# The second FFN layer of four pairs of token tiles as 2x2 block products with seven products instead of eight

## The chip, the cores and the metric

One core of a Trainium2 chip runs the program. It has five engines with queues of their own: PE (matmuls; PEld is its weight load), DVE (vector), ACT (activations), POOL (a second vector engine that reads and writes SBUF but not PSUM) and SP, which here only starts DMAs. The metric is the device time of one execution in microseconds (us); a difference of 0.3% (0.7 us) is about what a measurement can tell from no change.

## The reference

```
P = sort_net; five rounds of softmax over rows, then division by the column sums
k_sorted = einsum('bhij,bhjcd->bhicd', P, k_b)          # the same for v
attn = softmax(q_b @ k_sorted^T / 8);  x = attn @ v_sorted   # 32 groups of 96 tokens, 8 heads
h = x @ w_in                                            # 3072 x 512 by 512 x 2048
g = max(h, 0) + alpha * min(h, 0)
out = g @ w_out                                         # 3072 x 2048 by 2048 x 512, float32
```

## The kernel before

Tokens come in four batches of 768, each batch in eight groups of 96. For each group g attention is computed over all eight heads (`attention(g)`), for the next batch keys and values are mixed in between (`conv_k`, `prep_k`, `conv_v`, `prep_v`; the `conv` steps are copies into zero-padded tiles KSz and VDz, from the second batch on by POOL). Four groups make a chunk of 384 tokens. For each chunk `ffn1` computes 16 blocks of the hidden layer, one for each 128 of the 2048 columns: four matmuls of 384 columns into one of two PSUM banks (psH), an ACT instruction into a tile t1 (`t<-psH`), and a DVE instruction (SCALAR_TENSOR_TENSOR, STT below) that writes the block as bf16 into hT. hT is laid out [128 columns of the hidden layer, 16 blocks, ring of 768 tokens], so two chunks stand in it.

`ffn2` is the second layer. It works on tiles of 128 tokens, 24 in all. One tile is 16 matmuls that add up in one PSUM bank: the stationary operand is a 128x128 piece of hT, the moving one is a block row of w_out, 128 x 512. The bank is then copied to one of four tiles outstg by ACT or DVE, and SP stores it (256 KB). The banks are the two halves of psYP (keys psY and PSP), and the two of psS from tile 21 on. The last tile, 23, is made as two halves of 256 columns, in psS and psO, so that its last copy and store are short.

The order of work is not left to chance: every step is recorded in a graph (`_Graph.add`, with what it reads and writes), and the table `SEQ` holds one list of step numbers, with a letter where a step that several engines could do is given to one of them (p, a, d). `arrange` hands each engine its steps in that order; `emit` adds the semaphore waits. So each engine runs a fixed list, and an instruction that waits holds up everything behind it on its engine. The steps of the second layer come from `ffn_plan`, in the main part of the function.

Of the kernel before, what the change touches and what calls it, by code (L numbers as in the profile page):

```python
# [61 lines left out]
830 838 797 814 798 846 815d 818 799 839 844 800 831 845 804 819 821 820 864 822 771 848 865 772 832 874 849d  # L62
847 824 823 875 833 825 710 850 826 827 834d 851 872 648 828 805 852 873 829 883 853 675 866 854 876 855 877d
701 858 806 807d 856 878 867 884 859 879 860 885 773 857 840 898 841 880 835 899 861 774 881 944 882 862 900
863 892 842d 889 868 893 886 890 808 894 945 869 891 870 887d 756 924 895 925 901 912 896 926 897 888 913 871
906 843 909 950 910 902 951 739 907 946 903 914 908 952 927 911 918 904d 921 794 919 915 953 922 920 923 970
809 932 971 935 933 916d 947 936 934 972 937 981 938 928 973 939 941 940 996 942 982 905 943 958 997 961 959
929 948d 983 962 960 998 963 984 930d 964 985 967 999 1022 968 954 1023 965 1042 955 1010 969 1024 956d 1043
966 957 974 987 975 976d 931 978 988 1011 989 979 986 980 1048 949 993 1049 977 990 994 1012 995 991 917 992
1025 1007 1004 1008 1044 1009 1005 1050 1006 1019 1016 1000 1020 1013 1051 1001 1017 1021 1068 1018 1045 1002d  # L70
1033 1014d 1046 1003 1030 1069 1034 1026 1031 1079 1027 1035 1070 1032 1080 1028d 1039 1071 1036 1040 1081
1041 1037 1029 1038 1052 1059 1053 1054d 1082 1060 1055 1061 1056 1083d 1100 1057 1084 1058 1065 1047 1062
1066 1124 1067 1063 1064 1085 1072 1086 1076 1087 1125 1077 1073 1074 1078 1091 1088 1101 1092 1075 1089 1093
1126 1090 1015 1097 1094 1098 1102 1099 1095 1096 1109 1106 1110 1127 1111 1107 1108 1115 1112 1116 1103 1117
1113 1114 1121 1104d 1118 1122 1166 1119 1120 1172 1123 1130 1133 1131 1145 1134 1135 1146 1132 1139 1136 1140
1184 1141 1137 1167 1138 1151 1142 1152 1147 1153 1143 1144 1173 1128d 1157 1129 1154 1105 1158 1148 1159 1155
1156 1163 1149 1168 1150 1164 1165 1160 1185 1161 1174 1162 1186 1169 1187 1170 1175 1188 1189 1178 1171 1176
1179 1177 1180 1181 1182 1183
# [231 lines left out]
def bass_sinkhorn_attn__then__act_prelu_kernel(  # L310
# [48 lines left out]
    omaT = sb("omaT", [128, 16], F32)  # L359
# [111 lines left out]
    def consts():  # L471
# [6 lines left out]
        G.add(DVE, lambda e: e.memset(sel0[:, :, :], 0.0), 420, w=["sel0"], prio=-87)  # L478
# [24 lines left out]
        for n in range(NE):  # L503
# [19 lines left out]
        G.add(ACT, lambda e: copy(e, AP(selk, 0, [[512, 32], [16, 32], [1, 16]]),  # L523
                                  AP(identf, 0, [[128, 32], [1, 32], [0, 16]])), 600,
              r=["identf"], w=["selk"], prio=-66)
        G.add(ACT, lambda e: copy(e, AP(sel0, 0, [[1024, 32], [16, 8], [130, 8], [1, 2]]),
                                  AP(identf, 0, [[128, 32], [1, 8], [0, 8], [0, 2]])), 300,
              r=["identf"], w=["sel0"], prio=-66.5)
        return ib.idx
# [35 lines left out]
    def spread0(prio):  # L565
        def f(e):
            inst = None
            for j in range(8):
                inst = e.matmul(psYP[:, 1, 0:8], AP(sel0, j * 128, [[1024, 32], [1, 128]]),
                                AP(Pb, j, [[64, 32], [8, 8]]), start=(j == 0), stop=(j == 7))  # L570
            return inst
        G.add(PE, f, 300, r=["Pb", "sel0"], w=PSP, prio=prio)
        G.add(DVE, lambda e: e.tensor_tensor(
            out=AP(BDK, 0, [[512, 128], [16, 8], [2, 8], [1, 2]]),
            in0=AP(mkh, 0, [[16, 128], [2, 8], [0, 8], [1, 2]]),
            in1=AP(psYP, 512, [[1024, 128], [0, 8], [1, 8], [0, 2]]), op=AluOpType.mult), 330,
            r=PSP + ["mkh"], w=[("BDK", 0)], prio=prio)

    def spread(bs, prio):
        n = len(bs)  # L580
        late = bs[0] > 0
        rows = n * (1 + late)

        def f(e):
            inst = None
            for x in range(n):
                inst = e.matmul(psYP[:, 1, x * 64:x * 64 + 64], AP(selk, bs[x] * 128, [[512, 32], [1, 128]]), Pb[:, :])
            for x in range(n * late):
                for hf in range(2):
                    inst = e.matmul(AP(psYP, hf * 64 * 1024 + 512 + (n + x) * 64, [[1024, 64], [1, 64]]),  # L590
                                    AP(selk, bs[x] * 128, [[512, 32], [2, 64]]), Pb[:, :])
# [12 lines left out]
        for x, b in enumerate(bs):  # L604
            G.add(SMALL, lambda e, x=x, b=b: e.tensor_tensor(
                out=AP(BDM, b * 64, [[256, 128], [16, 4], [2, 8], [1, 2]]),
                in0=AP(mkhM, 0, [[8, 128], [2, 4], [0, 8], [1, 2]]),
                in1=AP(dsel, x * 8, [[48, 128], [0, 4], [1, 8], [0, 2]]), op=AluOpType.mult), {"dve": 220, "pool": 420},
                r=["dsel", "mkhM"], w=[("BDM", b)], prio=prio) if late else G.add(DVE, lambda e, x=x, b=b: e.tensor_tensor(
                out=AP(BDK, b * 128, [[512, 128], [16, 8], [2, 8], [1, 2]]),  # L610
                in0=AP(mkh, 0, [[16, 128], [2, 8], [0, 8], [1, 2]]),
                in1=AP(dsel, x * 8, [[48, 128], [0, 8], [1, 8], [0, 2]]), op=AluOpType.mult), 260,
                r=["dsel", "mkh"], w=[("BDK", b)], prio=prio)
        for x, b in enumerate(bs if late else []):
            G.add(SMALL, lambda e, x=x, b=b: e.tensor_tensor(
                out=AP(BDV, b * 64, [[256, 128], [8, 8], [1, 8]]),
                in0=AP(mkhV, 0, [[8, 128], [1, 8], [0, 8]]),
                in1=AP(dsel, (n + x) * 8, [[48, 128], [0, 8], [1, 8]]), op=AluOpType.mult), {"dve": 220, "pool": 420},
                r=["dsel", "mkhV"], w=[("BDV", b)], prio=prio + 0.5)
# [312 lines left out]
                  dma=(d_o[ob + x], 0))  # L932


    G.add(DVE, lambda e: e.memset(bz[:, :], 0.0), 100, w=["bz"], prio=-120)

    def burst(e):
# [41 lines left out]
    for ga, gb in chunks:  # L979
# [110 lines left out]
```

## Time and profile before

| | |
|---|---|
| runs | 234.4, 235.03, 235.07 us; median 235.03 |
| profiled execution | 232.5 us from its first to its last instruction; no other time of it is given |
| PE | busy 221.9 us (95%), 2516 matmuls recorded |
| weight loads | 139.3 us (60%) |
| DVE, ACT | 166.5 us (72%), 157.6 us (68%) |
| POOL | 102.7 us (44%), all of it before 141.4 us |
| granted TensorE clock | 1.000 |

A row of a group of instructions reads: line of the program, engine, operation, what it writes <- what it reads, sizes, count | busy us, mean ns of one | idle time of the engine before them and what ended it. The mean time of a matmul is its latency; matmuls overlap, so what one takes of PE is read from the distance of their starts.

### The profile page before, as it was taken

To read this page: it belongs to the slowest core of one execution; us is meant where nothing else is said; L and a number is where in the kernel's file an instruction comes from. 1 tells how busy PE (TensorE), PEld (TensorE's weight loads), DVE (VectorE), ACT (ScalarE), POOL (GpSimd) and SP (SyncE) were. 2 spreads that over 40 slices of the span, in tenths; PEclk is the share of its full clock that TensorE was granted. 3 is DMA by queue.
4 is the path that set the end of the run, shared out by engine and by line. 5 is a ranking of instruction groups with operands and counts; after the bars stand their busy time and mean duration, and the time that the engine had idled before them with its cause. 6 is when DMAs were issued, how large, how long until landed. Compare 5 with 4: busy or idle time off the path is not lost.

```text
span 232.5 us, 6278 instructions
## 1 busy us (share of the span) xinstructions
PE 221.9 (95%) x2516; PEld 139.3 (60%) x2543; DVE 166.5 (72%) x342; ACT 157.6 (68%) x435; POOL 102.7 (44%) x149
## 2 busy tenths in 40 slices
PE   3998999999999999999999999999999999999995
PEld 3456588685666656665665666555555555555553
DVE  5659599896898978696688677758677675463540
ACT  4369667889989596757888587686684764642332
POOL 7999239859076995863999932000000000000000
PEclk9999999999999999999999999999999999999999
DMA  5999999996996699999749998678515533200033
GB/s 70 218 209 197 215 205 186 184 192 116 192 183 124 64 123 170 172 193 206 155 104 137 107 110 181 131 178 171 97 34 143 116 57 121 63 0 0 10 128 135
DMA packets 73389, 31.36 MB, mean 135 GB/s; under 512 B 64512, under 2 KB 68368, under 8 KB 73360
## 3 DMA queue, kind: packets, MB, share of 16 engines
q0 software_dynamic: 24816, 13.63, 43.3%
q1 hardware_dynamic: 48544, 17.33, 37.1%
q8 instruction: 20, 0.33, 0.6%
q14 instruction: 9, 0.07, 0.1%
HBM read 27.28 MB, written 6.29 MB: 144 GB/s over the span
## 4 chain that ended last, share of the span: by engine, by line
PE 76%; POOL 11%; DMA 9%; issue 2%; ACT 0%; POOLq 0%
PE psH L875 32%; PE psYP L915 29%; DMA KS<-in_k_dram 9%; PE psS L915 4%; PE psS L756 3%; POOL KSz L655 3%; PE psO L813 3%; PE psYP L709 2%; PE psYP L668 2%; POOL VDz L401 1%; POOL QN L491 1%; POOL w_in_bf L960 1%; PE psO L915 1%; POOL QN L431 1%; PE psO L848 1%
## 5 line engine op out<-in xcount | busy, mean ns | idle before, releaser
L889 DVE SCALAR_TENSOR_TENSOR hT<-t,omaT,psH 128x384 bf16<-128x384 f32 (+1 forms) x140 | 76.7, 565 | 30.2 <-ACT t L885 29.4
L875 PE MATMUL psH<-xT,w_in_bf 128*128 128x384 bf16 (+1 forms) x560 | 96.9, 310 | 0.3 <-DVE hT L889 0.3
L885 ACT ACTIVATE t<-psH 128x384 f32<-128x384 f32 x126 | 60.6, 494 | 42.9 <-PE psH L875 42.3
L915 PE MATMUL psYP<-w_out_bf,hT 128*128 128x512 bf16 x309 | 78.4, 379 | 1.4
L875 PEld LDWEIGHTS psH<-xT,w_in_bf 128*128 128x128 bf16 x560 | 50.1, 98 | 29.2 <-DVE hT L889 2.7
L793 ACT ACTIVATE Esb<-psS,nf 96x96 bf16<-96x96 f32 x192 | 46.2, 344 | 2.1 <-DVE nf L765 2.0
L915 PEld LDWEIGHTS psYP<-w_out_bf,hT 128*128 128x128 bf16 x336 | 30.5, 98 | 28.1
L401 POOL COPY VDz<-VST 64x384 bf16<-64x384 bf16 x40 | 33.9, 848 | 16.4 <-PE psH L875 6.5
L655 POOL COPY KSz<-KS 64x512 bf16<-64x512 bf16 x36 | 22.1, 613 | 16.5 <-DMA KS<-in_k_dram 8.0
L765 DVE TENSOR_REDUCE nf<-psS 96x8 f32<-96x768 f32 x24 | 22.8, 950 | 8.9 <-PE psS L756 8.6
L431 POOL DMA_DIRECT2D QN<-in_q_dram x24 | 19.9, 846 | 0.7 <-POOL QN L491 0.6
L826 DVE TENSOR_TENSOR xq<-psO,rec 96x512 bf16<-96x512 f32 x27 | 18.4, 683 | 0.5
L813 PEld LDWEIGHTS psO<-VS,ET 112*128 112x128 bf16 x248 | 11.1, 98 | 3.4 <-ACT xT L401 0.5
L813 PE MATMUL psO<-VS,ET 112*128 112x65 bf16 x248 | 12.7, 194 | 0.0
L756 PEld LDWEIGHTS psS<-KT,QTz 128*128 128x128 bf16 (+1 forms) x192 | 10.7, 101 | 3.3 <-ACT Esb L793 0.2
L756 PE MATMUL psS<-KT,QTz 128*128 128x96 bf16 (+1 forms) x192 | 12.2, 206 | 0.0
L401 DVE CAST VS<-psYP 112x512 bf16<-112x512 f32 x15 | 10.3, 689 | 2.3 <-PE psYP L709 2.3
L821 DVE RECIPROCAL rec<-psO 96x8 f32<-96x8 f32 x31 | 6.2, 200 | 6.1 <-PE psO L813 5.7
L709 PEld LDWEIGHTS psYP<-BDV,VDz 128*128 128x128 bf16 x192 | 8.3, 98 | 3.3 <-POOL VDz L401 0.4
L401 ACT ACTIVATE outstg<-psYP 128x512 f32<-128x512 f32 x11 | 6.6, 603 | 5.0 <-PE psYP L915 4.9
L915 PE MATMUL psS<-w_out_bf,hT 128*128 128x512 bf16 (+1 forms) x48 | 9.8, 344 | 0.0
L709 PE MATMUL psYP<-BDV,VDz 128*128 128x64 bf16 x192 | 9.5, 193 | 0.1
(139 smaller groups left out, 209.6 us busy)
## 6 DMA issues: line engine op xcount, KB each, us to landing
out_dram<-outstg SPq DMA_DIRECT2D x23, 256.0 KB, 2.6
KS<-in_k_dram POOLq DMA_DIRECT2D x3, 768.0 KB, 9.1
QN<-in_q_dram POOLq DMA_DIRECT2D x24, 96.0 KB, 3.8
w_in_bf<-in_moe_w_in_dram POOLq DMA_DIRECT2D x4, 512.0 KB, 16.7
w_out_bf<-in_moe_w_out_dram POOLq DMA_DIRECT2D x2, 1024.0 KB, 18.5
VST<-in_v_dram POOLq DMA_DIRECT2D x4, 384.0 KB, 10.1
hT<-in_q_dram POOLq DMA_DIRECT2D x1, 768.0 KB, 7.3
VST<-in_v_dram POOLq DMA_DIRECT2D x1, 768.0 KB, 13.1
```

The source lines that it names most:

```text
L401: return e.activation(o, i, ACTF.Copy) if e is nc.scalar else e.tensor_copy(o, i)
L431: G.add(POOL, lambda e, h=h: e.dma_start(AP(QN, h * 128 + (h // 4) * 64, [[6144, 128], [1024, 6], [1, 64]]), AP(q.tensor, b * HB + h * S * ...
L655: G.add(POOL, lambda e, hp=hp: e.tensor_copy(AP(KSz, hp * 64 * 3072 + u % 3 * 1024 + hp * 64, [[3072, 64], [128, 8], [1, 64]]), AP(KS[n], ...
L709: inst = e.matmul(AP(t, off + dd * 64, [[row, 128], [1, 64]]), AP(VDz, (u % VSL * 8 + dd) * 128, [[VSL * 1024, 128], [1, 128]]), AP(BDV, b ...
L756: inst = e.matmul(o, AP(QTz[n], hp * 3072 + h4 * 768 + i * 96, [[6144, 128], [1, w]]), AP(KT[n], (h4 * 8 + i) * bk, [[ld, 128], [64, 2], [ ...
L765: G.add(DVE, lambda e: e.tensor_reduce(AP(nx, 0, [[8, 96], [4, 2], [1, 4]]), AP(psX, 0, [[1024, 96], [512, 2], [96, 4], [1, 96]]), AxisLis ...
L793: inst = e.activation(AP(Esb[me], p * 128, [[1024, 96], [64, 2], [1, 48]]), AP(psX, (p // 4) * 512 + (p % 4) * 96, [[1024, 96], [48, 2], [ ...
L813: inst = e.matmul(AP(psZ, hp * 512 + h4 * 68, [[1024, 128], [1, 65]]), AP(ET[me] if far else ET[m], pos(h4, hp) * 96, [[800, nk], [1, 128] ...
L875: inst = e.matmul(AP(pt, poff + x * n, [[1024, 128], [1, n]]), AP(w_in_bf, kt * DFF + (ft + x) * 128, [[KT_TILES * DFF, 128], [1, 128]]), ...
L885: G.add(ACT, lambda e: e.activation(AP(t1[tb], 0, [[384, 128], [1, k * n]]), AP(pt, poff, [[1024, 128], [1, k * n]]), ACTF.Relu, scale=-1. ...
L889: G.add(DVE, lambda e, x=x: e.scalar_tensor_tensor(out=AP(hT, (ft + x) * RING + tok % RING, [[FT_TILES * RING, 128], [1, n]]), in0=AP(t1[t ...
L915: inst = e.matmul(AP(bank[0], bank[1], [[1024, 128], [1, n]]), AP(hT, ft * RING + tok % RING, [[FT_TILES * RING, 128], [1, 128]]), AP(w_ou ...
```

## The change

Tiles 13+14, 16+17, 19+20 and 22+23 are taken as pairs a and b. For a pair the product is a 2x2 block product: the two tiles are the block rows; the even and the odd blocks of the hidden layer are the two halves of the inner dimension; the columns 0-255 and 256-511 of w_out are the block columns. Strassen's scheme (in Winograd's form) needs seven block products in place of eight. Each has eight matmuls of 256 columns, so a pair takes 56 matmuls of 256 columns where two tiles took 32 of 512.

For it there are four sums of blocks of w_out, made once (`w_sums`, eight instructions of 128x1024 bf16 elements, as each is cut in two halves), in SBUF that is free by then: KS[0] and VST[0], which held keys and values of the third batch, and a tile WT3, which takes the place of sel0 and selk and holds these until then. And for each pair there are four sums of blocks of hT (`strassen`, S1 to S4, eight instructions of 128x512 bf16), in QTz[0] or VDz. The seven products add up in psYP; in between its first quarter is copied to SBUF three times (`snap`) and added to other quarters on the way to outstg (`total`, DVE). The numbering of steps is new, and SEQ is new from about its last two fifths on, for all engines.

```diff
-775 783 777 811 784 786 778d 615 836 785 787 791 620 788 779 792 614 780d 837 617 795 793 781 616 796 770 782d
...
+775 783 777 811 784 786 778d 615 836 785 787 791 620 788 779 792 614 780d 837 795 781 804 793 782d 796 797 798
...
-    selk = sb("selk", [32, 4, 128], BF16)
+    WT3 = sb("WT3", [128, 8, 256], BF16)
...
-    sel0 = sb("sel0", [32, 8, 128], BF16)
...
+    PAIRS = [13, 16, 19, 22]
...
+    def wt(n, j):
+        if n == 3:
+            return WT3, 2048, j * 256
+        t, off = (((KS, VST)[n - 1][0], j * 256) if n < 3 else ((KS, VST)[j // 4][0], 2048 + j % 4 * 256))
+        return t, 3072, off
+
+    def w_sums():
...
+                G.add(SMALL, f, {"dve": 800, "pool": 2150},
+                      r=[("w_out", hf)] + [("WT", y, hf)] * isinstance(y, int),
+                      w=[("WT", n, hf)] + (["selk", "sel0"] if n == 3 else old[n - 1] if n < 3 else old[hf]),
+                      prio=-1)
...
+    def strassen(ta, prio):
...
+        for hf in range(2):
+            for n, x, y, op in ((1, (1, 0), (1, 1), AluOpType.add), (2, 1, (0, 0), AluOpType.subtract),
+                                (3, (0, 0), (1, 0), AluOpType.subtract), (4, (0, 1), 2, AluOpType.subtract)):
...
+                    return e.tensor_tensor(out=sv(n, hf), in0=i[0], in1=i[1], op=op)
+                G.add(SMALL, f, {"dve": 520, "pool": 1180}, r=r, w=[("S", m, n, hf)] + first, prio=prio + n / 100)
...
+        def snap(x):
+            G.add(EITHER, lambda e: copy(e, AP(sn, so + x * 256, [[sld, 128], [1, 256]]), AP(psYP, 0, [[1024, 128], [1, 256]])),
...
+        def total(o, n, off, x, keys):
+            G.add(DVE, lambda e: e.tensor_tensor(
+                out=o, in0=AP(psYP, off, [[1024, 128], [256, n], [1, 256]]),
+                in1=AP(sn, so + x * 256, [[sld, 128], [0, n], [1, 256]]), op=AluOpType.add),
...
+        product(0, ["psY"], True, ((0, 0), (0, 0)))
+        product(512, PSP, True, ((0, 1), (1, 0)))
+        snap(0)
+        total(outstg[oa][:, 0:256], 1, 512, 0, [("out", oa)])
+        product(0, ["psY"], False, (2, 2))
+        product(512, PSP, True, ((1, 1), 4))
+        product(768, PSP, False, (1, 1))
+        snap(1)
+        product(0, ["psY"], False, (3, 3))
+        snap(2)
+        total(outstg[ob][:, :], 2, 512, 2, [("out", ob), ("out", ob, 1)])
+        store(tb, ob)
+        product(768, PSP, False, (4, (1, 1)))
+        total(outstg[oa][:, 256:512], 1, 768, 1, [("out", oa, 1)])
+        store(ta, oa)
...
+            if tile_done + x in PAIRS:
+                ffn_plan.append((prios[0], 2, (tile_done + x, prios[0])))
+            if tile_done + x in PAIRS or tile_done + x - 1 in PAIRS:
+                continue
```

The diff's `SMALL` means DVE or POOL. By the new table POOL gets all eight sums of w_out and 25 of the 32 sums of hT, DVE the other seven. Up to the first engine's change the lists are the same: on PE for 231 rows, on DVE 211, on POOL 81.

On POOL, the end of the list before, from the last loads of Q (QN) on: the six copies of keys for the fourth batch.

```order
L655 COPY KSz<-KS1 64x8x64
L401 COPY VDz<-VST1 64x8x48
L655 COPY KSz<-KS1 64x8x64
L431 DMA QN<-in_q_dram 128x6x64 x5
L655 COPY KSz<-KS1 64x8x64 x6
```

The same place now; L957 is `w_sums`, L994 the sums of hT, here for the pair 13+14.

```order
L435 DMA QN<-in_q_dram 128x6x64 x5
L957 TENSOR_TENSOR KS0<-w_out_bf 128x1024
L659 COPY KSz<-KS1 64x8x64
L957 TENSOR_TENSOR KS0<-w_out_bf 128x1024
L659 COPY KSz<-KS1 64x8x64 x5
L994 TENSOR_TENSOR QTz0<-hT 128x512
L957 TENSOR_TENSOR VST0<-w_out_bf,KS0 128x1024
L957 TENSOR_TENSOR KS0<-w_out_bf,VST0 128x1024
L994 TENSOR_TENSOR QTz0<-hT 128x512
L957 TENSOR_TENSOR VST0<-w_out_bf,KS0 128x1024
L994 TENSOR_TENSOR QTz0<-hT,QTz0 128x512
L957 TENSOR_TENSOR VST0<-w_out_bf,VST0 128x1024
```

Two sums of w_out stand ahead of the copies of keys, and where POOL had nothing left it now goes on with sums, to near the end of the program.

On PE, the end of the list before (L875 is `ffn1`, L915 `ffn2`):

```order
L875 MATMUL psH<-xT,w_in_bf 128x384 x4
L915 MATMUL psO<-w_out_bf,hT 128x256 x4
L915 MATMUL psS<-w_out_bf,hT 128x512 x4
L915 MATMUL psO<-w_out_bf,hT 128x256 x4
L915 MATMUL psS<-w_out_bf,hT 128x512 x4
L915 MATMUL psO<-w_out_bf,hT 128x256 x4
L915 MATMUL psS<-w_out_bf,hT 128x512 x4
L915 MATMUL psS<-w_out_bf,hT 128x256 x16
```

The same place now, from the last `ffn1` on (L919 is `ffn2`, for tile 21; L1013 the products of the pair 22+23, whose sums of hT stand in VDz):

```order
L879 MATMUL psH<-xT,w_in_bf 128x384 x8
L1013 MATMUL psYP<-w_out_bf,hT 128x256 x4
L919 MATMUL psS<-w_out_bf,hT 128x512 x4
L1013 MATMUL psYP<-w_out_bf,hT 128x256 x12
L1013 MATMUL psYP<-VST,VDz 128x256 x8
L1013 MATMUL psYP<-KS,hT 128x256 x4
L1013 MATMUL psYP<-VST,hT 128x256 x4
L1013 MATMUL psYP<-WT,VDz 128x256 x8
L1013 MATMUL psYP<-KS,VDz 128x256 x8
L919 MATMUL psS<-w_out_bf,hT 128x512 x8
L1013 MATMUL psYP<-w_out_bf,VDz 128x256 x8
```

Half of tile 21 has moved to just before the last product.

On DVE, the end of the list before:

```order
L401 COPY outstg3<-psYP 128x512
L889 SCALAR_TENSOR_TENSOR hT<-t12,omaT,psH 128x384
L889 SCALAR_TENSOR_TENSOR hT<-t11,omaT,psH 128x384 x2
L889 SCALAR_TENSOR_TENSOR hT<-t10,omaT,psH 128x384
L401 COPY outstg3<-psO 128x256
```

The same place now, from the last two STTs on (COPY to KSz is a `snap`, L1027 a `total`):

```order
L893 SCALAR_TENSOR_TENSOR hT<-t10,omaT,psH 128x384
L893 SCALAR_TENSOR_TENSOR hT<-t11,omaT,psH 128x384
L994 TENSOR_TENSOR VDz<-hT 128x512
L405 COPY KSz<-psYP 128x256
L994 TENSOR_TENSOR VDz<-VDz,hT 128x512
L1027 TENSOR_TENSOR outstg2<-psYP,KSz 128x256
L405 COPY KSz<-psYP 128x256
L1027 TENSOR_TENSOR outstg3<-psYP,KSz 128x512
L994 TENSOR_TENSOR VDz<-hT,VDz 128x512
L405 COPY outstg1<-psS 128x512
L1027 TENSOR_TENSOR outstg2<-psYP,KSz 128x256
```

One short copy behind the last STT has become nine instructions, two of which (the first L994 and the first COPY) stand ahead of the first product of sums on PE. The last store is now a whole tile of 256 KB, where it was half a tile.

More of the change, by code (lines that the diff above doesn't have):

```diff
@@ L65 @@
[L65 to L74, printed above, removed]
@@ L477, in consts @@
                    prio=-84)
-        G.add(DVE, lambda e: e.memset(sel0[:, :, :], 0.0), 420, w=["sel0"], prio=-87)
+        G.add(DVE, lambda e: e.memset(AP(WT3, 512, [[2048, 32], [1, 1024]]), 0.0), 420, w=["sel0"], prio=-87)
         G.add(DVE, lambda e: e.memset(P32[:, 64:72], EPS), 100, w=["eps"], prio=-89)
@@ L522, in consts @@
               220, r=["one0"], w=[("VS1", 0)], prio=-60)
-        G.add(ACT, lambda e: copy(e, AP(selk, 0, [[512, 32], [16, 32], [1, 16]]),
+        G.add(ACT, lambda e: copy(e, AP(WT3, 0, [[2048, 32], [16, 32], [1, 16]]),
                                   AP(identf, 0, [[128, 32], [1, 32], [0, 16]])), 600,
               r=["identf"], w=["selk"], prio=-66)
-        G.add(ACT, lambda e: copy(e, AP(sel0, 0, [[1024, 32], [16, 8], [130, 8], [1, 2]]),
+        G.add(ACT, lambda e: copy(e, AP(WT3, 512, [[2048, 32], [16, 8], [130, 8], [1, 2]]),
                                   AP(identf, 0, [[128, 32], [1, 8], [0, 8], [0, 2]])), 300,
@@ L568, in f @@
             for j in range(8):
-                inst = e.matmul(psYP[:, 1, 0:8], AP(sel0, j * 128, [[1024, 32], [1, 128]]),
+                inst = e.matmul(psYP[:, 1, 0:8], AP(WT3, 512 + j * 128, [[2048, 32], [1, 128]]),
                                 AP(Pb, j, [[64, 32], [8, 8]]), start=(j == 0), stop=(j == 7))
@@ L586, in f @@
             for x in range(n):
-                inst = e.matmul(psYP[:, 1, x * 64:x * 64 + 64], AP(selk, bs[x] * 128, [[512, 32], [1, 128]]), Pb[:, :])
+                inst = e.matmul(psYP[:, 1, x * 64:x * 64 + 64], AP(WT3, bs[x] * 128, [[2048, 32], [1, 128]]), Pb[:, :])
             for x in range(n * late):
@@ L932, in ffn2, with f, at @@
                   dma=(d_o[ob + x], 0))
+    def wt(n, j):
[4 more added lines that the diff above has]
+    def w_sums():
+        w = lambda ft, h: AP(w_out_bf, ft * DM + h * 256, [[FT_TILES * DM, 128], [2 * DM, 4], [1, 256]])
+        old = [("KS", 0)], [("VST", 0)] + [("VST", 0, x) for x in range(4)]
+        for n, x, y, op in ((1, (0, 1), (0, 0), AluOpType.subtract), (3, (1, 1), (0, 1), AluOpType.subtract),
+                            (2, (1, 1), 1, AluOpType.subtract), (4, (1, 0), 2, AluOpType.subtract)):
+            for hf in range(2):
+                def f(e, n=n, x=x, y=y, hf=hf, op=op):
+                    def at(v):
+                        if isinstance(v, tuple):
+                            return w(8 * hf + v[0], v[1])
+                        t, ld, off = wt(v, 4 * hf)
+                        return AP(t, off, [[ld, 128], [256, 4], [1, 256]])
+                    return e.tensor_tensor(out=at(n), in0=at(x), in1=at(y), op=op)
+                G.add(SMALL, f, {"dve": 800, "pool": 2150},
+                      r=[("w_out", hf)] + [("WT", y, hf)] * isinstance(y, int),
+                      w=[("WT", n, hf)] + (["selk", "sel0"] if n == 3 else old[n - 1] if n < 3 else old[hf]),
+                      prio=-1)
@@ L997, in bass_sinkhorn_attn__then__act_prelu_kernel @@
                     ffn1(*a, pr)
+            elif kind == 2:
+                if a[0] == PAIRS[0]:
+                    w_sums()
+                strassen(*a)
             else:
```

81 lines of the change are left out of this document (73 added, 8 removed).

## The prediction

> **What bounds the kernel now.** I read the page first (engines, clock), then the stretch in which the lists differ, cut into stages, then the chain that ended last.
>
> ```profile
> span 232.5 us, 6278 instructions
> PE 221.9 (95%) x2516; PEld 139.3 (60%) x2543; DVE 166.5 (72%) x342; ACT 157.6 (68%) x435; POOL 102.7 (44%) x149
> core 0: us, PE busy (x) PEld busy (x) DVE busy (x) ACT busy (x) POOL busy (x), PEclk, DMA share, GB/s
> 134.00:160.00 26.00, 25.78 (x230) 15.44 (x233) 18.36 (x33) 20.09 (x72) 3.66 (x6) 1.00 0.79 149
> 160.00:180.00 20.00, 19.89 (x151) 11.49 (x152) 15.12 (x26) 12.48 (x39) 0.00 (x0) 1.00 0.47 107
> 180.00:200.00 20.00, 19.84 (x141) 11.22 (x143) 12.93 (x24) 12.59 (x40) 0.00 (x0) 1.00 0.37 87
> 200.00:229.70 29.70, 29.54 (x169) 16.58 (x170) 13.63 (x23) 11.25 (x23) 0.00 (x0) 1.00 0.15 53
> ```
>
> From 134 to 229.7 us PE is busy 95.06 of 95.70 us at full clock: it waits for 0.6 us in all, DVE and ACT have over a third of their time free, POOL almost all of it. So matmul time taken out of PE here shortens the run, as long as what is added to DVE, ACT and POOL comes in time. The chain at the end is PE alone:
>
> ```profile
> 199.91 1.73 PE psYP L915 x8
> 201.64 1.30 PE psH L875 x8
> 227.17 2.62 PE psS L915 x20
> ```
>
> Eight matmuls of 512 columns take 1.73 us (0.216 each), eight of 384 take 1.30 (0.163). The last 20 are 4 of 512 and 16 of 256: (2.62 - 4 x 0.216) / 16 = 0.110 for 256 columns.
>
> **PE.** The rows of the order behind the common part differ in two counts only. Before: 208 matmuls of 512 columns and 32 of 256 (tile 23). After: 96 of 512 and 224 of 256. That is -112 x 0.2157 + 192 x 0.1098 = -24.16 + 21.08 = **-3.08 us**, if PE waits no more than before. Per pair it is 56 x 0.110 against 32 x 0.216, 0.76 us; a little more for 22+23, where tile 23 was in halves. Each matmul still brings one weight load, so a pair has 56 instead of 32:
>
> ```profile
> L875 PEld LDWEIGHTS psH<-xT,w_in_bf 128*128 128x128 bf16 x560 | 50.1, 98 | 29.2 <-DVE hT L889 2.7
> ```
>
> 98 ns fit under 110, and the last 16 matmuls above, each with its load, show it. [...]
>
> **POOL, price of a sum.** POOL gets eight sums of 1024 elements and 25 of 512, two SBUF inputs each. No such instruction of this size is in the trace; the nearest rows:
>
> ```profile
> L655 POOL COPY KSz<-KS 64x512 bf16<-64x512 bf16 x36 | 22.1, 613 | 16.5 <-DMA KS<-in_k_dram 8.0 <-PE psYP L668 6.4
> L605 POOL TENSOR_TENSOR BDM<-mkhM,dsel 128x64 bf16<-128x64 f32 x2 | 0.6, 292 | 0.2
> L1075 POOL MEMSET const-bfloat16-1.0<- 128x1 bf16 x1 | 0.1, 110 | 0.0
> 129.70 4.09 POOL L431 DMA_DIRECT2D QN<-in_q_dram  x5
> 134.41 0.61 POOL L655 COPY KSz<-KS 64x512 bf16<-64x512 bf16 x1 [0.61 <-PE psYP L668]
> 138.03 3.30 POOL L655 COPY KSz<-KS 64x512 bf16<-64x512 bf16 x5 [3.01 <-PE psYP L668]
> 132.84 0.41 PE L813 MATMUL psO<-VS,ET 112*128 112x65 bf16 x8
> ```
>
> Below, a sum cannot be quicker than the copy of 512: 0.61 us. Above, the two-input row of 64 elements less a bare start of 0.11 gives 0.182 / 64 = 2.84 ns an element: 1.57 for 512, 3.02 for 1024. Between them: the copy costs (0.61 - 0.11) / 512 = 0.97 ns an element, two inputs twice that, and the 64-element row leaves 0.17 for the start: **1.16 and 2.16 us**. I take this, since it uses the operation's own row for the start and the row of the same size and type for the slope. [...]
>
> Does it come in time? POOL's loads end at 133.8. From there to the last sum of w_out stand 8 x 2.16 + 6 copies x 0.61 + 6 sums of pair 13+14 x 1.16 = 27.9 us: 161.7, and some 3 us more for blocks of hT not yet written. PE reaches WT3, the first use of that last sum, after 100 matmuls of 384 columns, 48 of 512, 40 of 256 and 152 short ones of attention (36.2 us by the spacings) from 132.84, where the lists part: 169.0. So 4 us are spare. The two sums that now stand ahead of copies of keys fill time in which POOL waited (0.61 and 3.01 us). Cost on PE: 0; above about 1.4 and 2.7 us a sum the cover is gone.
>
> **DVE and the port.** A pair's three copies and two of its totals have 256 elements (0.43 us on DVE, row below), one total has 512 (0.68): 2.8 us where two copies took 1.3. That, 1.5 us a pair on ACT and DVE together, and seven sums in all lie in a stretch where both have a third free; I count 0. What a DVE sum meets is another matter:
>
> ```profile
> 45.46 0.61 POOL L655 COPY KSz<-KS 64x512 bf16<-64x512 bf16 x1
> 45.77 0.38 DVE L615 TENSOR_TENSOR BDV<-mkhV,dsel 128x64 bf16<-128x64 f32 x1
> 39.27 0.89 POOL L965 DMA_DIRECT2D w_out_bf<-in_moe_w_out_dram  x1
> 39.35 0.22 DVE L605 TENSOR_TENSOR BDM<-mkhM,dsel 128x64 bf16<-128x64 f32 x1
> L889 DVE SCALAR_TENSOR_TENSOR hT<-t,omaT,psH 128x384 bf16<-128x384 f32 x37 | 21.8, 604 | 4.3 <-ACT t L885 4.2
> L889 DVE SCALAR_TENSOR_TENSOR hT<-t,omaT,psH 128x384 bf16<-128x384 f32 x60 | 35.7, 608 | 23.9 <-ACT t L885 23.4
> ```
>
> A DVE instruction with two SBUF inputs took 0.38 us and ended at 46.15, just behind POOL's copy (46.07); its twin beside a POOL DMA issue took 0.22. The STTs take 604 ns from 80 to 140 us, with POOL at work, and 608 after, without. So a DVE sum stands until POOL's instruction is over, and STTs do not care. [...]
>
> Where does that reach PE? At the end. Prices:
>
> ```profile
> L826 DVE TENSOR_TENSOR xq<-psO,rec 96x512 bf16<-96x512 f32 x27 | 18.4, 683 | 0.5
> L401 DVE COPY KT<-KT 128x512 bf16<-128x512 bf16 x1 | 0.3, 344 | 0.0
> L885 ACT ACTIVATE t<-psH 128x384 f32<-128x384 f32 x126 | 60.6, 494 | 42.9 <-PE psH L875 42.3
> L401 DVE COPY outstg<-psO 128x256 f32<-128x256 f32 x1 | 0.4, 425 | 1.9 <-PE psO L915 1.9
> L401 DVE COPY outstg<-psYP 128x512 f32<-128x512 f32 x10 | 6.8, 677 | 0.0
> ```
>
> A DVE sum of 512 lies between the SBUF copy, 0.34, and the two-input row that reads PSUM, 0.68; I take the middle, 0.52. Behind the last `ffn1` PE has 16 matmuls of 256 and 4 of 512 before the product VST,VDz: 2.62 us. On the other side: latency and hops 0.2, ACT 0.49, STT 0.61, to 1.33. POOL's sum of the block one STT earlier (0.65 before) runs until 0.57 past that, the DVE sum waits for it, then 0.52, then the copy to KSz 0.43: 1.33 + 0.57 + 0.52 + 0.43 = 2.85. PE waits **0.25 us**; none if the sum takes 0.34, 0.6 to 0.7 with 0.68, where the second sum is late too.
>
> **The tail.** Behind the last matmul:
>
> ```profile
> 227.01 2.77 PE L915 MATMUL psS<-w_out_bf,hT 128*128 128x512 bf16 x20
> 229.82 0.38 ACT L401 ACTIVATE outstg<-psS 128x256 f32<-128x256 f32 x1 [1.15 <-PE psS L915]
> DMA to landing us min/median/max: 1.7/2.1/3.7
> 201.14 29.42 SPq L929 DMA_DIRECT2D out_dram<-outstg  x8
> ```
>
> PE's last result is at 229.78, then come 0.38 on ACT and a store of 128 KB (the minimum of the last eight, 1.7). Now it is a total of 256 elements on DVE (0.43, as the copy of that size) and a store of 256 KB (2.1): **+0.44 us**; with a store at the minimum it would be +0.04. SP's list is dealt anew as well, its transposes and stores in nearly the old order; from 201 us on it has only stores, eight in 29 us, and POOL's sums come behind its last load, so I count no delay of a transfer.
>
> **Sum.** -3.08 + 0.25 + 0.44 = -2.4 on a span of 232.5, so 230.1. The runs' median is 2.5 above the span, and I leave that as it is: 235.03 - 2.4 = **232.6 us**. With 1.4 and 2.7 us for a POOL sum it becomes 233.7 (below); with no wait at the end and a quick store 231.9.
>
> **Rivals.** (1) POOL a little dearer, 1.3 to 1.45 us: DVE sums of pair 13+14 stand behind w_out sums of up to 2.7 us, the STTs behind them come late, and with two psH banks PE feels it: I estimate 0.6 to 0.9 us there, and 0.4 to 0.5 at the end. 233.1 to 234.3. For it: no row has the size. (2) POOL at its upper bound, 1.57 and 3.02; this is the slower one. The chain to WT3 is then 24.2 + 3.7 + 9.4 = 37.3 us, 171.1 without any wait, 2 late against 169.0; two DVE sums held by sums of 3.0 make about 1.8 us more by way of the STTs, the last pairs about 0.7. PE waits 4.5: -3.08 + 4.5 + 0.44 = +1.9, 236.9. It decides from about 1.5 and 2.85 us, where the waits reach 2.7 and the gain is gone. For it: the 64-element row; against it: that row has strided inputs in float32. (3) The seven products save nothing since weight loads set the pace: a load that did not hide would add 24 x 0.098 a pair, 2.35 - 0.76, so 235.03 + 4 x 1.6 + 0.7 = 242. The 16 matmuls at 0.110 speak against it. [...]
>
> **Chances.** Forecast (231.6 to 233.1) 0.66; rival 1 0.15; between rivals 1 and 2, no change, 0.06; rival 2 0.11; rival 3 0.02. Faster is the first two, 0.81; same 0.06; slower 0.13. A measurement tells 0.3% (0.7 us) from no change. The range goes from 231.6 (PE's whole gain, the tail as before, 0.3 to spare) to 234.6, which takes in rival 1.
>
> **What will show it.** PE should have 224 matmuls of 256 columns 0.110 apart and wait no more than 1 us from 134 on; POOL's TENSOR_TENSOR rows should read near 1160 and 2160 ns, and the last WT3 sum should end before 169; a DVE sum should end just behind a POOL sum at the end, with about 0.25 us of wait at the product VST,VDz; from the last matmul to the end it should be 3.1 us instead of 2.7. POOL sums over 1.4 us, or STTs that start late behind a DVE sum near 150 us, would make it wrong.

## The result and the profile after

| | before | after |
|---|---|---|
| runs | 234.4 to 235.07 us, median 234.78 of 4 | 231.42 to 232.06 us, median 231.75 of 4 |
| ratio | | 0.9866, 95% interval 0.9846 to 0.9886 |
| profiled execution, span | 232.5 us | 229.7 us |

The change makes the kernel 1.3% faster; 232.6 us (231.6 to 234.6) was forecast. The page of the changed kernel (engines over the whole span), and below it the four stages that the prediction showed of before: stretch, length, busy time (and count) of PE, PEld, DVE, ACT and POOL, granted clock, DMA share, GB/s.

```profile
span 229.7 us, 6502 instructions
PE 220.6 (96%) x2623; PEld 147.1 (64%) x2623; DVE 175.4 (76%) x362; ACT 154.6 (67%) x416; POOL 148.2 (65%) x182
134.00:160.00 26.00, 26.00 (x240) 15.77 (x239) 20.45 (x38) 19.84 (x63) 21.79 (x17) 1.00 0.82 146
160.00:180.00 20.00, 20.00 (x187) 14.22 (x186) 16.62 (x31) 14.45 (x48) 11.60 (x10) 1.00 0.51 114
180.00:200.00 20.00, 20.00 (x162) 13.59 (x160) 14.69 (x27) 10.49 (x27) 4.46 (x4) 1.00 0.28 66
200.00:226.60 26.60, 26.60 (x195) 18.71 (x192) 16.28 (x31) 9.61 (x20) 11.54 (x10) 1.00 0.16 61
```

PE is busy in every moment from 134 us to its last matmul, at full clock. POOL, almost idle there before, is at work for 49 us of it, and PE never waits for it.

Two traces are compared best from a point that both have. Such a point, some way ahead of the first difference on PE, is a group of attention, eight matmuls `psS<-KT,QTz`. PE's timeline, start and length: the point in before and in after, and PE's last row after (before it is the row of 20 matmuls that the prediction shows).

```profile
119.56 0.50 PE L756 MATMUL psS<-KT,QTz 128*128 128x96 bf16 x8
119.63 0.50 PE L760 MATMUL psS<-KT,QTz 128*128 128x96 bf16 x8
225.60 1.04 PE L1013 MATMUL psYP<-w_out_bf,VDz 128*128 128x256 bf16 x8
```

From that point PE needs 110.22 us before and 107.01 after: 3.21 saved. From its last result to the end of the span it is 2.69 before and 3.10 after: 0.41 lost. What is left is -2.80 of the span's -2.73; the other 0.07 lies ahead of the point.

The same three numbers for every kernel below, in us. The ratio is to runs of before on the same chip (medians 234.56 to 234.79); of half_store_free_port a run at a mean clock of 0.985 is left out, and products_128_wide has two runs only. Comparisons go by the second column, since the first moves by over 1 us from run to run (119.41 to 120.75), in waits ahead of the change (PE waited 0.6 us for POOL's copies to VDz in eight_products, for none of them in after).

| kernel | point | PE from there | behind PE | runs, median | ratio to before (95%) |
|---|---|---|---|---|---|
| before | 119.56 | 110.22 | 2.69 | 234.78 | |
| after | 119.63 | 107.01 | 3.10 | 231.75 | 0.9866 (0.9846 to 0.9886) |
| eight_products | 120.59 | 110.50 | 3.10 | 235.58 | 1.0027 (1.001 to 1.0043) |
| short_sums | 120.19 | 107.01 | 3.10 | 231.92 | 0.9882 (0.9853 to 0.9911) |
| sums_in_two | 120.47 | 107.01 | 3.10 | 232.07 | 0.9886 (0.9861 to 0.9911) |
| sums_in_four | 120.75 | 109.24 | 3.10 | 234.34 | 0.9974 (0.9957 to 0.9991) |
| sums_as_rival_1 | 120.30 | 108.89 | 3.1 | 233.85 | 0.9964 (0.9944 to 0.9985) |
| sums_as_rival_2 | 120.68 | 111.91 | 3.1 | 237.66 | 1.013 (1.0091 to 1.0169) |
| rival_1_own_waits | 120.65 | 107.6 | 3.1 | 232.65 | 0.9904 (0.9871 to 0.9938) |
| rival_2_own_waits | 119.41 | 112.7 | 3.1 | 236.87 | 1.0092 (1.005 to 1.0134) |
| free_port | 120.14 | 107.01 | 3.10 | 232.08 | 0.9899 (0.9862 to 0.9937) |
| half_store | 120.25 | 107.01 | 2.80 | 231.62 | 0.9865 (0.983 to 0.99) |
| half_store_free_port | 119.81 | 107.01 | 2.80 | 231.82 | 0.9875 (0.984 to 0.991) |
| products_128_wide | 120.03 | 107.57 | 3.08 | 232.31 | 0.9898 (0.9843 to 0.9952) |

### The profile page after: what moved, and what is told of

Same layout as the page of the kernel before. It is cut to its first block, busy times and chain, and to the rows that moved or that the text cites. A ratio compares the mean times of both kernels' runs of the same rounds, so it can differ in the third digit from the quotient of the medians.

```text
span 229.7 us, 6502 instructions
## 1 busy us (share of the span) xinstructions
PE 220.6 (96%) x2623; PEld 147.1 (64%) x2623; DVE 175.4 (76%) x362; ACT 154.6 (67%) x416; POOL 148.2 (65%) x182
## 4 chain that ended last, share of the span: by engine, by line
PE 76%; POOL 11%; DMA 9%; issue 1%; DVE 0%; POOLq 0%
PE psH L879 32%; PE psYP L919 21%; PE psYP L1013 11%; DMA KS<-in_k_dram 9%; PE psS L760 3%; POOL KSz L659 3%; PE psO L817 3%; PE psYP L713 2%; PE psYP L672 2%; PE psS L919 2%; POOL VDz L405 1%; POOL QN L495 1%; POOL w_in_bf L1077 1%; POOL QN L435 1%; PE psO L852 1%
## 5 line engine op out<-in xcount | busy, mean ns | idle before, releaser
L919 PE MATMUL psYP<-w_out_bf,hT 128*128 128x512 bf16 x240 | 60.2, 379 | 0.0
L919 PEld LDWEIGHTS psYP<-w_out_bf,hT 128*128 128x128 bf16 x240 | 21.6, 98 | 19.4
L830 DVE TENSOR_TENSOR xq<-psO,rec 96x512 bf16<-96x512 f32 x30 | 20.5, 684 | 0.7
L994 POOL TENSOR_TENSOR QTz<-hT 128x512 bf16<-128x512 bf16 x7 | 8.1, 1156 | 16.5 <-DVE hT L893 15.7
L994 POOL TENSOR_TENSOR VDz<-hT 128x512 bf16<-128x512 bf16 x7 | 8.1, 1153 | 15.6 <-DVE hT L893 15.3
L405 ACT ACTIVATE outstg<-psYP 128x512 f32<-128x512 f32 x12 | 7.2, 601 | 4.4 <-PE psYP L919 4.4
L405 ACT ACTIVATE KT<-psYP 128x512 bf16<-128x512 f32 x13 | 7.8, 598 | 3.2 <-PE psYP L672 3.0
```

Of the source, the lines that this page charges most:

```text
L405: return e.activation(o, i, ACTF.Copy) if e is nc.scalar else e.tensor_copy(o, i)
L919: inst = e.matmul(AP(bank[0], bank[1], [[1024, 128], [1, n]]), AP(hT, ft * RING + tok % RING, [[FT_TILES * RING, 128], [1, 128]]), AP(w_ou ...
```

## The experiments

### Is the gain the seventh of the matmuls? eight_products

The first product of each pair is issued twice, so that a pair has 64 matmuls of 256 columns and all else stays.

```diff
-                        inst = e.matmul(AP(psYP, off, [[1024, 128], [1, 256]]), sa, mb,
-                                        start=begin and j == 0, stop=j == 7, skip_group_check=True)
+                        for again in range(1 + (reads == ((0, 0), (0, 0)))):
+                            inst = e.matmul(AP(psYP, off, [[1024, 128], [1, 256]]), sa, mb,
+                                            start=begin and j == 0 and not again, stop=j == 7, skip_group_check=True)
```

> The changed kernel with the first of a pair's seven products issued twice, so that PE has the work of eight products of 256 columns while every other instruction and the order stay (the output has that product twice). Theory (PE's matmul time is all that counts): 32 matmuls more at 0.109 us, +3.5 us on the changed kernel's 231.75, so 235.2, at or just above the kernel before. Rival (the gain comes from the new lists, that is from shorter waits, not from fewer matmuls): the time stays well below the kernel before, 232 to 233.5.

PE's timeline in this kernel, the common point and the last row:

```profile
120.58 0.50 PE L760 MATMUL psS<-KT,QTz 128*128 128x96 bf16 x8
230.05 1.04 PE L1014 MATMUL psYP<-w_out_bf,VDz 128*128 128x256 bf16 x8
```

110.50 us (from the unrounded times): 3.49 more than the changed kernel, which is 32 x 0.109. Every matmul put in or taken out here is paid in full, nothing absorbs it. And the new order with eight products is 0.28 slower on PE than before (64 x 0.109 a pair against 32 x 0.2157, with tile 23 of before in halves, makes 0.26), so the new layout of the lists brings nothing by itself: the gain is the missing product. The runs agree: 0.28 us and the 0.41 behind PE are 0.3% (1.0027 measured).

### What do the sums cost? short_sums, and the sums cut in pieces

In `short_sums` the sums of hT and six of the eight sums of w_out are made for 32 elements in place of 512 or 1024 (the two into WT3 stay whole). The other kernels cut POOL's sums in pieces; each further piece adds 0.14 us (times below). In the kernels with pieces only POOL's instructions change.

```diff
# short_sums, the sums of hT; those of w_out likewise, but for WT3
-                    return e.tensor_tensor(out=sv(n, hf), in0=i[0], in1=i[1], op=op)
+                    cut = lambda a: AP(a.tensor, a.offset, [a.ap[0], a.ap[1], [1, 8]])
+                    return e.tensor_tensor(out=cut(sv(n, hf)), in0=cut(i[0]), in1=cut(i[1]), op=op)
...
# sums_in_two (k = 2), sums_in_four (k = 4), the sums of hT; those of w_out likewise
-                    return e.tensor_tensor(out=sv(n, hf), in0=i[0], in1=i[1], op=op)
+                    k = 2 if e is nc.gpsimd else 1
+                    for p in range(k):
+                        o, a, b = (AP(v.tensor, v.offset + p * (4 // k) * v.ap[1][0], [v.ap[0], [v.ap[1][0], 4 // k], v.ap[2]])
+                                   for v in (sv(n, hf), i[0], i[1]))
+                        inst = e.tensor_tensor(out=o, in0=a, in1=b, op=op)
+                    return inst
```

> The changed kernel with all sums of hT and six of the eight sums of w_out cut to 8 of each 128 or 256 columns, on POOL and DVE (the rest of the sums is left out, so the output differs). Theory (the sums are hidden, but for nothing or little at the end): 231.75, no more than 0.2 us faster. [...]

> The changed kernel with each POOL sum made as two instructions of half the size, which pays the fixed part of about 0.18 us once more: 1.34 and 2.31 us in place of 1.15 and 2.12. Theory (4 us spare at WT3; only the DVE sum at the end stands behind a longer POOL sum): +0.1 to +0.3 us, 232.0. Rival (POOL's chain has no slack): 25 x 0.18 + 8 x 0.18, up to +6 us.

> The changed kernel with each POOL sum made as four instructions of a quarter of the size: 1.70 and 2.67 us. Theory (rival 2 of the prediction, POOL too dear): the sums come late for PE near 151, 165, 211 and 224 us, PE waits about 4 us in all, 235.8, so no gain or a small loss against the kernel before. Rival (DVE and PE have more slack than counted): 232 to 233.

POOL's groups, of the changed kernel (two rows) and of `sums_in_four` (two rows): count, busy us, mean ns, idle time before them.

```profile
L994 POOL TENSOR_TENSOR QTz<-hT 128x512 bf16<-128x512 bf16 x7 | 8.1, 1156 | 16.5 <-DVE hT L893 15.7 <-DVE QTz L994 0.6
L957 POOL TENSOR_TENSOR WT<-w_out_bf 128x1024 bf16<-128x1024 bf16 x2 | 4.3, 2126 | 0.2
...
L1003 POOL TENSOR_TENSOR QTz<-hT 128x128 bf16<-128x128 bf16 x28 | 11.0, 425 | 13.8 <-DVE hT L893 13.3
L961 POOL TENSOR_TENSOR WT<-w_out_bf 128x256 bf16<-128x256 bf16 x8 | 5.1, 670 | 0.2
```

A whole sum takes 1.16 and 2.13 us. The same sums from POOL's timeline, one kernel each: in two pieces 1.29 to 1.30 and 2.28, in four 1.58 and 2.55 (pieces overlap a little, so these are less than their rows' sums: four times 425 ns make 1.70, four times 670 make 2.68).

```profile
151.70 2.28 POOL L961 TENSOR_TENSOR VST<-w_out_bf,KS 128x512 bf16<-128x512 bf16 x2
154.05 1.29 POOL L1003 TENSOR_TENSOR QTz<-hT,QTz 128x256 bf16<-128x256 bf16 x2
...
153.41 2.55 POOL L961 TENSOR_TENSOR VST<-w_out_bf,KS 128x256 bf16<-128x256 bf16 x4
156.03 1.58 POOL L1003 TENSOR_TENSOR QTz<-hT,QTz 128x128 bf16<-128x128 bf16 x4
```

PE's time does not move, to 0.01 us, when most of the sums' work is taken away, nor when they take 0.15 us more: hidden altogether, where 0.1 to 0.3 us had been expected of the two pieces. With four pieces PE loses 2.23 us, where about 4 had been expected. Its waits there, by what PE waited for and how long:

```profile
PE psYP L1023 <- DVE QTz L405: 1.5, 1, 1.5
PE psYP L1023 <- POOL QTz L1003: 0.4, 1, 0.4
```

One wait of 1.5 us at 164.5 us, at the product VST,QTz of pair 13+14, for a DVE copy; one of 0.4 at 210.7 us, at the same product of pair 19+20, for a sum. None near 151 us and none at the end, where the prediction's rivals had put some. A wait is counted from the modelled end of the matmul ahead of it. The next matmul of a row starts 0.16 us before that end (eight of 384 columns take 1.46 us where their starts alone, 0.163 apart, make 1.30), so PE loses 0.16 us more than each wait: 1.9 + 2 x 0.16 makes 2.2 of the 2.23.

### The rivals at their own prices: sums_as_rival_1, sums_as_rival_2

The same cutting, unequal, so that the sums take what the rivals assumed: three and five pieces for rival 1's upper corner, four and seven for rival 2.

```diff
+                    for b, k, c, l in [(0, 2, 0, 128), (2, 1, 0, 128), (3, 1, 0, 128)]:   # rival 1, hT; w_out: 256 x 3, 128 x 2
+                        o, x_, y_ = (AP(v.tensor, v.offset + b * v.ap[1][0] + c, [v.ap[0], [v.ap[1][0], k], [1, l]])
+                                     for v in (sv(n, hf), i[0], i[1]))
+                        inst = e.tensor_tensor(out=o, in0=x_, in1=y_, op=op)
```

> POOL's sums of hT are cut in three (256, 128, 128 elements) and those of w_out in five, so that with the 0.14 us which each further piece took in the runs before (1.30 and 2.28 us in two pieces, 1.58 and 2.55 in four) they take about 1.44 and 2.69 us: the upper corner of rival 1. The prediction's rival 1 expects 0.6 to 0.9 us of waits near 150 us and 0.4 to 0.5 at the end, 1.0 to 1.4 more on PE than the changed kernel. The theory from the four pieces, that POOL's chain to the last sum of pair 13+14 may come 1.05 us later than its 2.85 in that run less the wait of 1.8, expects 6 x 0.28 + 6 x 0.57 less POOL's 2.6 us of idle time, 2.5 us late, so one wait of about 1.4 us at 163 us, none near 150 and none at the end.

> POOL's sums of hT are cut in four and those of w_out in seven pieces, by the same count about 1.58 and 2.98 us: rival 2's own prices (1.57 and 3.02). Rival 2 expects PE to wait 4.5 us more than in the changed kernel and the kernel to be slower than before, by 1.9 us. The theory from the four pieces expects the chain of pair 13+14 another 6 x 0.43 = 2.6 us later than in four pieces, 1.8 + 2.6 = 4.4 us of wait at 163 us, and 0.6 at 207 us as there: 5.0 us more on PE, 2.2 us slower than before. If POOL were no bound at all, nothing would be added.

In `sums_as_rival_1` the sums took 1.44 and 2.69 us and PE lost 1.88; in `sums_as_rival_2` 1.58 and 2.98, and PE lost 4.90 (in each, two sums of w_out that met a DVE sum took 0.2 to 0.4 us longer). The waits of PE in the second, and the DVE copy behind the first of them, with its idle time:

```profile
PE psYP L1025 <- DVE QTz L405: 3.6, 1, 3.6
PE psYP L1025 <- POOL QTz L1005: 0.4, 1, 0.4
PE psYP L672 <- POOL KSz L659: 0.4, 1, 0.4
168.16 0.42 DVE L405 COPY QTz<-psYP 128x256 f32<-128x256 f32 x1 [4.28 <-POOL QTz L1005]
```

So rival 2 was a real danger: at its prices the kernel is 1.3% slower than before (0.9 to 1.7%). Its size was about right (4.5 against 4.90), its place was not: it is nearly all one wait, of a copy of PSUM (`snap`), in front of which DVE stands 4.28 us for POOL's last sum of the pair.

### Why does a copy wait for the last sum? rival_1_own_waits, rival_2_own_waits

The copy does not use the sums. In the code of `strassen` both write `first`, the list of the old contents of the memory that they take over; so for the first two pairs all sums and copies are recorded as writers of all of it, and each waits for the one recorded before. These kernels are the two just shown with that chain cut: every sum and copy waits for the old contents' last readers, and for nothing of each other that it doesn't read (`old` is the list that was `first`).

```diff
...
+            before_it = {G.last_w[k] for k in old if k in G.last_w}.union(*(G.reads.get(k, ()) for k in old))
...
-                G.add(SMALL, f, {"dve": 520, "pool": 1180}, r=r, w=[("S", m, n, hf)] + first, prio=prio + n / 100)
+                G.add(SMALL, f, {"dve": 520, "pool": 1180}, r=r, w=[("S", m, n, hf)], prio=prio + n / 100).deps.update(before_it)
...
-                  t_either(256), r=["psY"], w=[("sn", m, x)] + first, prio=prio)
+                  t_either(256), r=["psY"], w=[("sn", m, x)], prio=prio).deps.update(before_it)
```

> As sums_as_rival_1, but the first two pairs' sums and copies wait only for the last readers of the memory that they take over, each by itself; in the changed kernel they are also chained to one another, since all of them are recorded as writers of that whole memory, so that the first copy to SBUF waits for the pair's last sum. Theory: the wait of 1.7 us at 163 us came from this chain, and goes; next due is WT3, whose last sum ended at 170.7 us there and which PE reaches at 169.1 + 0.7 in the changed kernel's order, its second half 0.4 us later: a wait of about 0.5 us is left of the 1.9 us. Rival: PE waited for the sums themselves, and the 1.9 us stay.

> As sums_as_rival_2, with the chain among the first two pairs' sums and copies taken out in the same way. Theory: the wait of 3.6 us at 163 us goes, and WT3 takes its place: its last sum ended at 174.2 us there, PE would reach it at about 171.0, so about 3.1 us, with the 0.4 us at 207 us and the 0.4 us behind POOL's copies of keys left: 4.1 us more on PE than in the changed kernel instead of 4.9. Rival: the sums of hT themselves are late at 163 us; then the wait there stays at 3.6 us.

PE's waits, first of `rival_1_own_waits` (its only one), then of `rival_2_own_waits`:

```profile
PE psYP L1026 <- POOL WT L962: 0.4, 1, 0.4
...
PE psYP L1026 <- POOL WT L962: 2.7, 2, 2.4
PE psYP L1026 <- POOL QTz L1006: 0.4, 1, 0.4
PE psYP L672 <- POOL KSz L659: 0.3, 1, 0.3
```

The wait of the copy is gone in both, and WT3 is late in its place, as expected; with the sums at rival 2's prices it makes 2.7 us of waits, where the prediction's chain to WT3 came 2 late. In the first kernel PE loses 0.59 us (0.5 expected) where it lost 1.88, so the rest was the chain of writers. In the second the waits make 3.4 us, with 0.16 more for each of the four 4.0, where 4.1 was expected; but PE loses 5.7. Behind the wait of 2.4 us the granted clock falls to 0.50, for 3.41 us. First its timeline of PE; then its stretches around the fall of the clock and, for comparison, two of `sums_as_rival_2` around its wait of 3.6 us (the first bracket is PE, the third number from the right the clock):

```profile
172.74 0.61 PE L1026 MATMUL psYP<-WT,QTz 128*128 128x256 bf16 x4 [2.36 <-POOL WT L962]
173.79 2.76 PE L879 MATMUL psH<-xT,w_in_bf 128*128 128x384 bf16 x8
178.04 1.46 PE L879 MATMUL psH<-xT,w_in_bf 128*128 128x384 bf16 x8
169.81:173.22 3.41, 1.05 (x9) 0.70 (x10) 0.91 (x2) 0.12 (x1) 3.27 (x9) 1.00 0.46 89
173.22:176.63 3.41, 3.41 (x23) 2.03 (x21) 1.55 (x2) 0.92 (x3) 3.25 (x10) 0.50 0.00 0
...
163.31:166.73 3.42, 1.70 (x12) 0.89 (x10) 0.57 (x2) 2.39 (x10) 3.26 (x9) 1.00 0.47 125
166.73:170.14 3.41, 1.50 (x19) 1.39 (x20) 1.98 (x5) 0.00 (x0) 3.33 (x9) 1.00 0.29 54
```

Eight matmuls of 384 columns take 2.76 us at a clock of 0.50 and 1.46 at 1.00. By the starts of the rows, 173.19 to 176.73, the half clock cost 1.65 us, which is what the waits leave open. Six of this kernel's ten runs had a mean clock of 0.986 to 0.993 and took 236.8 to 238.7 us, the four at 0.998 and above 235.2 to 235.7.

### The end: free_port, half_store, half_store_free_port

In `free_port` POOL's last sum goes to DVE, behind the first copy; so the DVE sum ahead of that copy meets no work on POOL. In `half_store` the first half of tile 22, which is ready 5.6 us before PE's last result, gets a store of its own, so the last store is 128 KB instead of 256.

```diff
# free_port: the order
-1240p 1249 1247 1250
+1249 1247 1240 1250
# half_store
+            c = 256 * (t == 22)
-            G.add(SYNC, lambda e: e.dma_start(AP(out.tensor, t * 128 * DM, [[DM, 128], [1, DM]]), outstg[o][:, :]),
+            G.add(SYNC, lambda e: e.dma_start(AP(out.tensor, t * 128 * DM + c, [[DM, 128], [1, DM - c]]), outstg[o][:, c:]),
...
+    G.add(SYNC, lambda e: e.dma_start(AP(out.tensor, 22 * 128 * DM, [[DM, 128], [1, 256]]), outstg[2][:, 0:256]),
+          1900, r=[("out", 2)], w=[("outd", 22, 0)], prio=99, dma=(d_o[4], 0))
```

> The changed kernel with POOL's last sum of hT (which overlaps the DVE sum of the last pair) given to DVE, behind the total of 256. Theory (the DVE sum of 0.83 us stood 0.41 us behind POOL's): that row falls to 0.42 us; PE, for which the copy came just in time, gains 0 to 0.1 us. Rival (the 0.83 us have another cause, such as two STTs just ahead): the row stays at 0.83.

> The changed kernel with tile 22's store in two halves: columns 0 to 255, ready at 221 us, are stored then, and only 128 KB are left behind the last total. Theory (the tail grew by 0.37 us, mostly because the last store is twice as large): 0.3 to 0.4 us faster than the changed kernel, 231.4 where it has 231.75; from the last matmul to the end 2.7 us. Rival (the store's size is not what its time hangs on): no change.

> Both edits, of the store in halves and of POOL's last sum on DVE. Theory: as the store in halves, 231.3 to 231.4; a version a little better than the changed kernel. Rival: no change, 231.75.

The end of the changed kernel, its timeline (start, length) from PE's first row behind the last `ffn1` on, and how long its last eight stores took from issue to landing:

```profile
217.78 0.60 PE L1013 MATMUL psYP<-w_out_bf,hT 128*128 128x256 bf16 x4
218.54 1.15 POOL L994 TENSOR_TENSOR VDz<-hT 128x512 bf16<-128x512 bf16 x1 [5.08 <-DVE hT L893]
219.15 0.83 DVE L994 TENSOR_TENSOR VDz<-hT 128x512 bf16<-128x512 bf16 x1
219.90 0.41 DVE L405 COPY KSz<-psYP 128x256 f32<-128x256 f32 x1
220.38 1.04 PE L1013 MATMUL psYP<-VST,VDz 128*128 128x256 bf16 x8
226.68 0.42 DVE L1027 TENSOR_TENSOR outstg<-psYP,KSz 128x256 f32<-128x256 f32 x1 [0.18 <-PE psYP L1013]
227.13 0.33 SPq L1033 DMA_DIRECT2D out_dram<-outstg  x1
DMA to landing us min/median/max: 2.0/2.1/2.3
```

The same DVE sum and copy in `free_port`, and the landing of the last stores in `half_store`, of which two are of 128 KB:

```profile
219.66 0.42 DVE L945 TENSOR_TENSOR VDz<-hT 128x512 bf16<-128x512 bf16 x1
220.22 0.42 DVE L356 COPY KSz<-psYP 128x256 f32<-128x256 f32 x1
...
DMA to landing us min/median/max: 1.7/2.0/2.3
```

Beside POOL's sum the DVE sum takes 0.83 us and ends at 219.98, 0.29 behind POOL's 219.69; without it 0.42, as do the other six DVE sums of the changed kernel (0.41 to 0.42), none of which meets a sum of POOL. So the doubling goes with POOL's sum, as the prediction said. The 0.29 are 0.13 less than the sum's own 0.42, so the sum's own time does not begin only when POOL's is over, as the forecast had counted. Yet PE's time is the same within 0.01 us: the copy ends at 220.31, and PE comes to its product at 220.38. The smaller last store takes 0.30 us off the end (2.80 against 3.10 behind PE), in both kernels that have it. These two are the best versions found by the trace, 109.8 us from the common point to the end against 110.1; the runs cannot tell them from the changed kernel (0.9865 and 0.9875 against 0.9866).

### Narrower still: products_128_wide

Each matmul of 256 columns is issued as two of 128, each with its own weight load: 448 instead of 224.

```diff
+                        for c in range(2):
+                            inst = e.matmul(AP(psYP, off + c * 128, [[1024, 128], [1, 128]]), sa,
+                                            AP(mb.tensor, mb.offset + c * 128, [mb.ap[0], [1, 128]]),
+                                            start=begin and j == 0 and c == 0, stop=j == 7, skip_group_check=True)
```

> The changed kernel with each matmul of the products as two of 128 columns, each with its own weight load: 448 of 128 columns in place of 224 of 256. Theory (loads hide behind matmuls of 128 columns too, as the 30 ns from start to start in the groups of 64 columns show): 448 x 0.056 against 224 x 0.109, +0.7 us, 232.4. [...]

PE loses 0.56 us (0.7 expected): (224 x 0.109 + 0.56) / 448 = 0.0558 us for 128 columns. Two rows of PE's timeline show it directly, 16 matmuls from one start to the next in 0.90 us:

```profile
223.03 1.06 PE L1014 MATMUL psYP<-WT,VDz 128*128 128x128 bf16 x16
223.93 1.06 PE L1014 MATMUL psYP<-KS,VDz 128*128 128x128 bf16 x16
```

So loads hide at half the width too, at 56 ns a matmul with a load of its own, and rival 3 is excluded with room to spare.

## Why the prediction was right

- **PE, -3.08.** Measured -3.21, with no wait left over. The chain of the changed kernel shows the spacing directly, 12 matmuls of 256 columns in 1.31 us:

```profile
190.12 1.31 PE psYP L1013 x12
```

  0.109 in place of 0.1098 gives -24.16 + 20.93 = -3.23. That the whole count is paid was argued from PE being busy; `eight_products` showed it. One reading on the way was wrong: the 0.6 us for which PE was said to wait before are no waits. They are 12 gaps of 52 to 56 ns, each where a matmul of `ffn2` has no record in the trace, as here, in the trace of before, with four loads and three matmuls:

```profile
137.77 0.56 PEld L915 LDWEIGHTS psYP<-w_out_bf,hT 128*128 128x128 bf16 x4
138.01 0.81 PE L915 MATMUL psYP<-w_out_bf,hT 128*128 128x512 bf16 x3
```

  From 134 to 229.7 us 693 loads stand against 681 matmuls. So there was no waiting to save, and the count alone had to give the gain.
- **POOL, 1.16 and 2.16, cost on PE 0.** Measured 1.16 and 2.13, and nothing. The cover is thinner than its price suggests: WT3 was done at 165.91 and PE reached it at 169.07 (169.0 forecast), 3.2 us spare of the 4 forecast.

```profile
160.34 1.15 POOL L994 TENSOR_TENSOR QTz<-hT,QTz 128x512 bf16<-128x512 bf16 x1
161.58 4.33 POOL L957 TENSOR_TENSOR WT<-w_out_bf 128x1024 bf16<-128x1024 bf16 x2
163.27 1.04 PE L1013 MATMUL psYP<-VST,QTz 128*128 128x256 bf16 x8
169.07 1.04 PE L1013 MATMUL psYP<-WT,QTz 128*128 128x256 bf16 x8
```

  What the step missed is an earlier date: the chain of writers, at the product VST,QTz. POOL's last sum of the pair ended at 161.49, and PE came to the product at 163.27. In `sums_as_rival_2` 0.58 us lie between the two, for the copy, so about 1.2 us were spare there. It cost nothing as the sums came out.
- **The end, +0.25 of wait.** It did not come. POOL's sum ended where it was expected, 1.91 us behind the last `ffn1` (217.78 to 219.69; 1.33 + 0.57 forecast, though the terms given for these add up to 1.30 and 0.51; latency and hop to ACT, counted as 0.2, took 0.19, from 217.78 to 217.97), and the DVE sum beside it did take longer, 0.83 us. The term that was mis-sized is what follows, DVE sum and copy: 0.62 us where 0.52 + 0.43 was counted. The sum took 0.42 by itself and ended only 0.29 behind POOL's, and the copy began before the sum was over. So the copy was done 0.07 us before PE came.
- **The tail, +0.44.** Measured +0.41. Of this 0.30 is the size of the store (`half_store`), where 0.40 was counted, and 0.04 the total on DVE (0.42) in place of a copy on ACT (0.38); the other 0.07 is not taken apart.
- **From span to runs, 2.5 us.** This is the larger error: the changed kernel's median is 2.0 above its profiled span. The median of three runs was set beside one profiled execution. In all runs of before that were timed later with their spans, the time is 1.7 to 1.8 us more than the span, and runs with a span of 232.5 took 234.24 and 234.28. So the profiled execution was one of the quick ones. The steps made the span 0.4 too long (230.1 for 229.7), the offset adds 0.5: together the 0.9 between 232.6 and 231.75. No error hid another: each step erred to the slow side.
- **The rivals.** Rival 1 at its upper corner costs 1.88 us (1.0 to 1.4 forecast), at 1.30 and 2.28 nothing. Rival 2 costs 4.90 (4.5 forecast) and ends on the slow side. The gain is gone when PE waits 2.80; that lies between 1.58 and 2.55 (2.23) and 1.58 and 2.98 (4.90), where each us on a w_out sum costs 6.2 us. At the forecast's point of 1.5 and 2.85 us an estimate is 2.23 + 6.2 x 0.30, less about 6 x 0.08 for the six sums of hT in the chain: 3.6. So the turn is a little earlier than "about 1.5 and 2.85". Of the mechanism, STTs behind DVE sums with two psH banks, no run shows a wait over 0.2 us.

## What to carry to other kernels

Where one engine is busy 99% of a stretch, count what the change takes from and adds to it and price it by the spacing in a row of equal instructions; that alone gave 3.08 of 3.21 us. Before the last per cent is called waiting, compare the matmuls with the weight loads: records can be missing (12 of 693 here). Work that moves to an idle engine is free until its last due date (PE took 107.01 us with POOL's sums whole, cut short and in two pieces), so look for the earliest date, and for dates that come from bookkeeping: a dependence through a shared list of "old contents" left 1.2 us to spare, where the next date, one that the data set, left 3.2. And put the profiled execution's own time, not the median of other runs, beside its span.

## What the runs showed of the hardware that was not expected

- POOL's sum of two bf16 inputs takes about 0.19 us and 1.9 ns an element from 512 to 1024 elements (1.16, 2.13), as two copies' slopes had suggested.
- A wait of PE can cost more than its length. In `rival_2_own_waits` the granted clock was 0.50 for 3.41 us (173.22 to 176.63) behind a wait of 2.36 us, and that cost PE another 1.65 us; six of its ten runs had a mean clock of 0.986 to 0.993, the other four of 0.998 and above. Behind the longer wait of `sums_as_rival_2`, 3.63 us, the clock stayed at 1.00. What decides whether it falls was not shown.
